# Local and global attention with a three-way max layer: the first 16 tiles written stage by stage and issued in that order, large tiles at one place modulo 256 bytes

## The chip, the cores and the metric

The kernel runs on one core of a Trainium2 chip. The metric is the device time of one execution in microseconds (us). Before the change three runs took 868.49, 871.20 and 872.62 us, median 871.2. One more execution was recorded by the hardware profiler.

## The reference

For 8 batches and 8 heads of width 64 there are 512 local tokens and 32 global ones. A global token attends to all 544 tokens, a local one to the 32 global tokens and to the local tokens within 32 positions. Two softmaxes, one output, then a layer with three first matrices and a maximum over them:

```python
s_g = scale * np.matmul(q_g, k_all.transpose(0, 1, 3, 2))
out_g = np.matmul(sm(s_g), v_all)
s_ll = np.where(np.abs(pos[:, None] - pos[None, :]) <= 32, scale * q_l @ k_l.T, -1e9)
s_l = np.concatenate([s_lg, s_ll], axis=-1)
out_l = np.matmul(sm(s_l), np.concatenate([v_g, v_l], axis=2))
x = concat([out_g, out_l], axis=2) -> [8 * 544, 512]
h = np.maximum(np.maximum(x @ w1, x @ w2), x @ w3)      # 512 -> 768
out = h @ w_out                                         # 768 -> 512
```

All inputs and outputs are fp32.

## The kernel before

A *tile* `sl` is 128 local queries of one pair of heads: 4 tiles (`t` = 0 to 3) make a pair `p`, 4 pairs a batch `b`, so there are 128 tiles, 16 to a batch. The work on one tile has these stages:

- `scores` (lines 290 to 322): four matmuls of queries and keys into PSUM (L305 for the first 28 tiles, L309 later); on DVE, for each of the two heads, a fused mask, scale and row minimum that reads PSUM (L312); on ACT the exponential with its row sum (L314); on DVE 1e-9 added and the reciprocal (L316, L317); the scaling `times` (mostly on POOL, L110); and a DMA that lays the result into `early` or `prob` (L320).
- `trans` (L332): four PE transposes of that tile into PSUM `T`, copied to `pt` by ACT or DVE.
- `transg` (L350): one transpose of the global softmax, copied into the same `pt`.
- `pv` (L370, later L377): the matmuls with the values into PSUM `O`, copied to `xr`; after the fourth tile of a pair a sum over `xr` (L387).
- `glob`, `glob_soft`: once a pair, the scores of the global queries in two halves (L263, L271), their softmax (L279 to L282) and six DMAs into `probg` (L288).
- `split_x`: once a pair, `xr` is split into a rounded part and its remainder, `xs` (a copy on ACT or DVE, a subtraction on POOL or DVE, L92).

`moe_group` is the dense layer of one batch: for each of six column blocks `f`, 36 matmuls of 512 columns (L408: rounded weights `wh` with both parts of `xs`, remainders `wl` with the first), then the maximum on DVE (L416) and a split `h`; then 72 matmuls with `woh` and `wol` (L427). The generator `fill(n)` puts n of these matmuls between the stages of the tiles of the *next* batch, 18 to a tile. So the layer of batch 0 runs beside tiles 16 to 31.

The weights come as 64-bit numbers in 24 pieces (18 of w1 to w3, then 6 of w_out). `convert` makes one piece into its two parts: an absolute value on ACT (L165), four DVE instructions over 512 columns (L166 to L169), a rounded copy `wh` on DVE or ACT and a subtraction `wl` on POOL. `weight_step` advances two pieces by one of these phases each and starts the DMA of another; the list `WS` says how many such steps follow each tile.

The names `copy`, `sub` and `times` choose the engine by counts of spent nanoseconds (`least`), at lines 98 and 100, 92, and 106 to 110. The order in which an engine's instructions stand is not the order of the program text: the framework's scheduler sorts what the text issues, by a model of when it can start. Each engine then works through its queue in order.

PSUM has 8 banks: three for `pm` (the dense layer, and the scores of the first 12 tiles), two for `S` (other scores, `transg`, `glob`), one for `T` and two for `O`. In SBUF most large tiles begin 32 bytes past a multiple of 256; the ones that are allocated after the small tiles `nm` and `z` begin 160 bytes past.

Of the kernel before, what the change touches and what calls it, by code (L numbers as in the profile page):

```python
# [51 lines left out]
def body(ctx, tc, kin, qin, vin, min_, w1, w2, w3, w4, out):  # L52
    nc = tc.nc
    act, dve, pool, pe = nc.scalar, nc.vector, nc.gpsimd, nc.tensor
# [8 lines left out]
    psO = ctx.enter_context(tc.tile_pool(name="psO", bufs=1, space=PSUM))  # L63

# [51 lines left out]
    mask = const.tile([128, 2, 224], BF16, name="mask")  # L116
    zero = const.tile([128, 1], F32, name="zero")
# [38 lines left out]
    def convert(piece):  # L156
# [3 lines left out]
        nc.sync.dma_start(out=r.rearrange("p (k f) -> p k f", k=k) if k > 1 else r, in_=src)  # L160
# [39 lines left out]
    EARLY, AHEAD = 16, 9  # L200
    kraw, kst, qraw, qs, vraw, vs, xr, sc, pg, pts = [{} for _ in range(10)]

    def load_k(p):
        if p < B * NP:
            if 4 * p in NATK:
                kraw[p] = att.tile([128, KW + 2 * SG], F32, name="kn", tag="kst")
            else:
                kraw[p] = att.tile([128, KW + 2 * SG], F32, name="kraw", bufs=1)
            nc.sync.dma_start(out=kraw[p], in_=kin[p])
# [15 lines left out]
    def load_q(s):  # L225
        if s < NS:
# [4 lines left out]
            nc.sync.dma_start(out=qraw[s], in_=qin[s])  # L231
# [8 lines left out]
    def load_v(s):  # L240
        if s < NS:
            vraw[s] = att.tile([128, 4, D], F32, name="vraw", bufs=3)
            nc.sync.dma_start(out=vraw[s], in_=vin[s].rearrange("p (x d) -> p x d", d=D))
# [8 lines left out]
    def glob(p, step):  # L252
        if p >= B * NP:
            return
        if step == 0:
            pg[p] = [att.tile([64, NG], F32, name="sg", bufs=1), att.tile([64, 2], F32, name="nmg"), att.tile([64, 2], F32, name="zg")]
# [3 lines left out]
        ps = psS.tile([128, 512], F32, name="S")  # L260
# [4 lines left out]
        else:  # L265
            for j in range(2):
# [4 lines left out]
        dve.tensor_tensor_reduce(out=s[:, s0:s0 + n], in0=ps[0:64, 0:n], in1=in1, scale=-0.125, scalar=3.0e38,  # L271
                                 op0=ALU.add, op1=ALU.min, accum_out=nm[:, step:step + 1])
        spend("d", n * 1.04 + 75)

    def glob_soft(p):
# [4 lines left out]
        act.activation(out=s, in_=s, func=AF.Exp, bias=nm[:, 0:1], scale=-1.0, accum_out=z[:, 0:1])  # L280
        dve.tensor_scalar(out=z[:, 0:1], in0=z[:, 0:1], scalar1=1e-9, scalar2=None, op0=ALU.add)
        dve.reciprocal(out=z[:, 0:1], in_=z[:, 0:1])  # L282
        spend("d", 220)
        spend("a", 760)
        times(s, s, z[:, 0:1])

        for c0, n, i, h, d0 in GPUT:
            nc.sync.dma_start(out=f32(probg[p % 2])[64 * h:64 * h + 64, i, d0:d0 + n], in_=s[:, c0:c0 + n])  # L288

    def scores(sl):  # L290
        if sl >= NS:
            return
# [3 lines left out]
        ps = pm.tile([128, 512], F32, name="pm") if sl < 12 else psS.tile([128, 512], F32, name="S")  # L296
        s = att.tile([128, 2, 224], F32, name="s", bufs=4)
        sc[sl] = early[:, sl % 6] if sl < EARLY else prob[sl % 2]
        nm = att.tile([128, 2], F32, name="nm")
        z = att.tile([128, 2], F32, name="z")  # L300
        ph = [ps[:, 0:224], ps[:, 224:448]]
        for j in range(2):
# [5 lines left out]
            for a in range(2):  # L308
                pe.matmul(ph[j][:, 0:n], lhsT=qs[sl][:, a, 128 * j:128 * j + 128],  # L309
                          rhs=kst[p][:, j, c0:c0 + n], start=(a == 0), stop=(a == 1))  # L310
        for j in range(2):
# [3 lines left out]
                           accum_out=z[:, j:j + 1])  # L315
        dve.tensor_scalar(out=z, in0=z, scalar1=1e-9, scalar2=None, op0=ALU.add)  # L316
# [3 lines left out]
        nc.sync.dma_start(out=f32(sc[sl])[:, :, 0:n], in_=s[:, :, 0:n])  # L320
        spend("d", 2 * (n * 1.04 + 75) + 150)
        spend("a", 2 * (n * 0.833 + 278))
# [115 lines left out]
    def moe_local(b):  # L438
        def st(t, o):
            r = b * TOK + SG + t * 128  # L440
            nc.sync.dma_start(out=out[r:r + 128], in_=o)
        return moe_group(xs.pop(b), SL, st)

    def moe_glob():
        t = [split_x(xg[:, k], 256) for k in range(NP)]

        def st(i, o):
            for c in range(4):
                r = (4 * i + c) * TOK
                nc.sync.dma_start(out=out[r:r + SG], in_=o[32 * c:32 * c + 32])  # L450
# [4 lines left out]
    WS = [0, 0, 0, 1, 0, 1, 0, 1, 0, 1, 0, 1, 2, 2, 1, 2, 2, 1, 2, 2, 1, 2, 2, 1, 2, 2]  # L455
# [8 lines left out]
    def next_scores(last):  # L464
        while ahead[0] <= last:
            scores(ahead[0])
# [3 lines left out]

    load_k(0)
    load_q(0)
    mraw = cut[:, 5, 0:448].bitcast(F32)
    nc.sync.dma_start(out=mraw, in_=min_.rearrange("p t c -> p (t c)"))
    dve.tensor_copy(out=mask.rearrange("p t c -> p (t c)"), in_=mraw)
    load_q(1)
    load_q(2)
# [101 lines left out]
```

## Time and profile before

| | |
|---|---|
| three runs | 868.49, 871.20, 872.62 us (median 871.2) |
| the profiled execution | 873.07 us |
| its span, first to last instruction | 871.3 us |
| PE busy, and idle in the span | 817.7 us (94%), 53.6 us |
| DVE, ACT, POOL busy | 614.3, 492.2, 504.6 us |

A profile is read here by its stages. "Busy" is the time in which at least one instruction of the engine runs. PEld is the loading of the stationary operand, which overlaps PE. A row of a timeline holds the start, the length, the engine, the source line, the operation, its output and inputs, and in brackets the idle time of the engine just before it and what ended that. PEclk is the share of TensorE's full clock that was granted. Line numbers are those of the kernel before.

### The profile page before, as it was taken

How to read it: one execution, taken by the hardware profiler on the slowest of the kernel's cores; microseconds unless marked ns; L12 is line 12 of the kernel's file. 1: busy time of each engine (PE TensorE's matmuls, PEld its weight loads, DVE VectorE, ACT ScalarE, POOL GpSimd, SP SyncE). 2: the span in 40 equal slices, each digit the busy share in tenths (PEclk: the TensorE clock that was granted, in tenths of full speed). 3: DMA queues.
4: the chain of work that ended last, by engine and by line, in shares of the span. 5: the costliest groups of instructions: out<-in, count | busy, mean ns of one | idle time of the engine just before them, and what ended most of it. 6: DMA issues, size and time to landing. Idle time of an engine off the chain costs nothing.

```text
span 871.3 us, 15748 instructions
## 1 busy us (share of the span) xinstructions
PE 817.7 (94%) x4452; PEld 674.0 (77%) x4452; DVE 614.3 (71%) x1885; ACT 492.2 (56%) x1392; POOL 504.6 (58%) x669
## 2 busy tenths in 40 slices
PE   5875788899999999999999999999999999999997
PEld 4553566688888888888888888888888888888896
DVE  5577788887778787887788887877887877521111
ACT  4555455566666666666676667676666665411111
POOL 4444666685667666776667566756676664411211
PEclk8798799899999999999999999999999999999999
DMA  6567564534333533343334423353334321100001
GB/s 215 172 191 220 176 209 129 160 95 142 100 99 103 164 104 110 99 136 118 95 103 120 134 90 109 90 158 110 104 110 135 117 85 61 69 15 1 25 25 25
DMA packets 107239, 98.54 MB, mean 113 GB/s; under 512 B 21008, under 2 KB 97936, under 8 KB 107152
## 3 DMA queue, kind: packets, MB, share of 16 engines
q1 hardware_dynamic: 107152, 97.53, 36.8%
q8 instruction: 36, 0.59, 0.3%
q14 instruction: 51, 0.42, 0.2%
HBM read 56.85 MB, written 8.91 MB: 75 GB/s over the span
## 4 chain that ended last, share of the span: by engine, by line
PE 79%; DVE 9%; DMA 4%; POOL 3%; issue 3%; ACT 1%; SPq 0%; DVEq 0%; ACTq 0%; POOLq 0%
PE pm L408 46%; PE pm L427 14%; PE O L377 6%; PE S L309 5%; PE T L332 4%; DMA wraw<-w_in 2%; PE S L267 1%; PE S L305 1%; PE O L370 1%; DMA wraw<-wo_in 1%; DVE wraw L168 1%; POOL wl L92 1%; PE S L350 1%; DVE xs L98 1%; DMA early<-s 1%
## 5 line engine op out<-in xcount | busy, mean ns | idle before, releaser
L408 PE MATMUL pm<-xs,wh 128*128 128x512 f32 (+1 forms) x1296 | 412.6, 391 | 16.1 <-POOL xs L92 8.8
L408 PEld LDWEIGHTS pm<-xs,wh 128*128 128x128 f32 x1296 | 234.7, 190 | 52.4 <-POOL xs L92 10.5
L408 PE MATMUL pm<-xs,wl 128*128 128x512 f32 (+1 forms) x648 | 255.1, 394 | 0.5 <-POOL wl L92 0.5
L110 POOL TENSOR_SCALAR s<-s,z 128x224 f32<-128x224 f32 (+1 forms) x243 | 110.0, 465 | 89.1 <-ACT lox L100 48.7
L314 ACT ACTIVATE s<-s,nm 128x192 f32<-128x192 f32 (+1 forms) x256 | 118.0, 462 | 51.2 <-DVE nm L312 26.9
L408 PEld LDWEIGHTS pm<-xs,wl 128*128 128x128 f32 x648 | 123.4, 190 | 24.1 <-issue 1.0
L427 PE MATMUL pm<-woh,h 128*128 128x512 f32 x408 | 136.0, 401 | 1.2 <-POOL h L92 1.1
L92 POOL TENSOR_TENSOR h<-m,h 128x512 fp32r<-128x512 f32 (+1 forms) x54 | 69.0, 1278 | 96.2 <-ACT h L100 96.2
L92 POOL TENSOR_TENSOR qs<-qraw,qs 128x256 fp32r<-128x256 f32 x100 | 78.7, 787 | 69.1 <-ACT qs L100 40.4
L416 DVE TENSOR_TENSOR m<-pm,m 128x512 f32<-128x512 f32 (+1 forms) x108 | 71.0, 658 | 65.5 <-PE pm L408 65.4
L92 DVE TENSOR_TENSOR pt<-T,pt 128x512 fp32r<-128x512 f32 x102 | 70.4, 691 | 34.3 <-ACT pt L100 32.4
L427 PEld LDWEIGHTS pm<-woh,h 128*128 128x128 f32 x408 | 74.7, 188 | 16.0 <-POOL h L92 4.3
L312 DVE CUSTOM_DVE_ANT_0 s<-S,mask 128x192 f32<-128x192 f32 (+1 forms) x232 | 77.6, 370 | 12.1 <-PE S L305 7.7
L427 PE MATMUL pm<-wol,h 128*128 128x512 f32 x204 | 82.0, 402 | 0.0
L92 POOL TENSOR_TENSOR vs<-vraw,vs 128x256 fp32r<-128x256 f32 x102 | 75.8, 743 | 8.9 <-ACT vs L100 3.9
L100 ACT CAST pt<-T 128x512 fp32r<-128x512 f32 x83 | 48.6, 586 | 47.7 <-PE T L332 47.5
L377 PEld LDWEIGHTS O<-pt,vs 128*128 128x128 f32 x408 | 66.9, 188 | 9.1
L377 PE MATMUL O<-pt,vs 128*128 128x320 f32 (+1 forms) x408 | 73.4, 301 | 0.0
L100 ACT CAST qs<-qraw 128x256 fp32r<-128x256 f32 x85 | 34.5, 406 | 65.6 <-PE S L309 61.9
L309 PEld LDWEIGHTS S<-kst,qs 128*128 128x128 f32 x400 | 59.7, 190 | 11.5 <-DVE nmg L271 2.8
L316 DVE TENSOR_SCALAR z<-z 128x2 f32<-128x2 f32 x128 | 40.6, 317 | 38.0 <-ACT s L314 34.7
L100 ACT CAST h<-m 128x512 fp32r<-128x512 f32 (+1 forms) x54 | 32.3, 598 | 61.1 <-DVE m L416 61.0
(99 smaller groups left out, 1344.8 us busy)
## 6 DMA issues: line engine op xcount, KB each, us to landing
vraw<-v_in SPq DMA_DIRECT2D x128, 128.0 KB, 2.4
qraw<-q_in SPq DMA_DIRECT2D x100, 128.0 KB, 2.2
prob<-s SPq DMA_DIRECT2D x56, 224.0 KB, 2.5
prob<-s SPq DMA_DIRECT2D x56, 192.0 KB, 2.3
wraw<-w_in SPq DMA_DIRECT2D x18, 512.0 KB, 4.8
out_dram<-o SPq DMA_DIRECT2D x32, 256.0 KB, 2.5
kraw<-k_in SPq DMA_DIRECT2D x25, 320.0 KB, 3.0
qn<-q_in SPq DMA_DIRECT2D x28, 128.0 KB, 3.1
```

Of the source, the lines that this page charges most:

```text
L92: (dve if least(c) == "d" else pool).tensor_tensor(out=out, in0=a, in1=b, op=ALU.subtract)
L100: act.copy(out=out, in_=a)
L110: pool.tensor_scalar(out=out, in0=a, scalar1=col, scalar2=1.0, op0=ALU.mult, op1=ALU.mult)
L309: pe.matmul(ph[j][:, 0:n], lhsT=qs[sl][:, a, 128 * j:128 * j + 128], rhs=kst[p][:, j, c0:c0 + n], start=(a == 0), stop=(a == 1))
L312: dve.tensor_tensor_reduce(out=s[:, j, 0:n], in0=ph[j][:, 0:n], in1=mask[:, (1, 0, 1, 0)[t], 32 * (t == 0):32 * (t == 0) + n], scale=-0.12 ...
L314: act.activation(out=s[:, j, 0:n], in_=s[:, j, 0:n], func=AF.Exp, bias=nm[:, j:j + 1], scale=-1.0, accum_out=z[:, j:j + 1])
L316: dve.tensor_scalar(out=z, in0=z, scalar1=1e-9, scalar2=None, op0=ALU.add)
L332: pe.transpose(pr[:, 256 * j + 128 * c:256 * j + 128 * c + 128], s[:, j, 128 * c:128 * c + 128], identr)
L377: pe.matmul(o[:, j, 0:320].rearrange("p (a q) -> p a q", a=2)[:, :, 0:n], lhsT=vs[sl][:, 2 * j + c].rearrange("p a d -> p (a d)"), rhs=pt[ ...
L408: pe.matmul(ps[:, 0:n], lhsT=w[f][:, i, k], rhs=xs[k][:, a, 0:n], start=(q == 0), stop=(q == 11))
L416: dve.tensor_tensor(out=m[:, 0:n], in0=ps[:, 0:n], in1=m[:, 0:n], op=ALU.max)
L427: pe.matmul(ps, lhsT=hh[f][:, a, 128 * t:128 * t + 128], rhs=w[:, f], start=(q == 0), stop=(q == 17))
```

## The change

It has two parts.

The first is an order. Every engine handle becomes an `Engine` object. While `strict[0]` is true it keeps each instruction on its engine in the order of the text, and it remembers the last instruction of each engine. `scores` is cut into `score_products` (the matmuls), `score_exp` (mask, minimum, exponential) and `score_norm` (reciprocal, scaling, DMA), `glob_soft` into `glob_exp` and `glob_norm`, and the DVE half of `glob` can be put off through the list `later`. The loop over the first 16 tiles is written anew. At tile `sl` it issues the transposes of tile `sl+1`, then `step()` (normalise the tile whose exponentials were issued one step before, exponentials of the tile whose products were issued last, then the put-off halves of `glob`), the products of tile `sl+5`, `weight_step`s, the values of tile `sl`, `glob`, and the global transpose of tile `sl+1`. After the 16 tiles `strict[0]` becomes false, and everything later is placed behind the last strict instruction of its engine (`issue_after`). So no matmul of the dense layer can stand ahead of the end of this block. The scores of the first 16 tiles and their `glob` take their PSUM from `pm`; 20 tiles instead of 16 use `early`. `WS` has 10 steps instead of 12 in the first 16 tiles, and 16 instead of 17 from tile 16 on.

The second part is a place. The small tiles `nm`, `z`, `nmg`, `zg` and `zero` move to a pool `small` at the end of SBUF, with four buffers instead of two for the first four; `mask` is padded to 256 columns and `sg` to 576. All large tiles then begin 128 bytes past a multiple of 256.

```diff
+    strict = [True]
+    last = {}
+    class Engine:
...
+            def g(*args, **kw):
+                i = f(*args, **kw)
+                if strict[0]:
+                    tc.keep_in_program_order(i)
+                    last[self.name] = i.ins
+                return i
...
+    small = ctx.enter_context(tc.tile_pool(name="small", bufs=4))
-    mask = const.tile([128, 2, 224], BF16, name="mask")
+    mask = const.tile([128, 2, 256], BF16, name="mask")
-    EARLY, AHEAD = 16, 9
+    EARLY = 20
-        ps = psS.tile([128, 512], F32, name="S")
+        ps = pm.tile([128, 512], F32, name="pm") if later is not None else psS.tile([128, 512], F32, name="S")
-        ps = pm.tile([128, 512], F32, name="pm") if sl < 12 else psS.tile([128, 512], F32, name="S")
+        ps = pm.tile([128, 512], F32, name="pm") if sl < 16 else psS.tile([128, 512], F32, name="S")
-        nm = att.tile([128, 2], F32, name="nm")
-        z = att.tile([128, 2], F32, name="z")
+        nm = small.tile([128, 2], F32, name="nm")
+        z = small.tile([128, 2], F32, name="z")
-    WS = [0, 0, 0, 1, 0, 1, 0, 1, 0, 1, 0, 1, 2, 2, 1, 2, 2, 1, 2, 2, 1, 2, 2, 1, 2, 2]
+    WS = [0, 0, 1, 1, 1, 0, 1, 1, 1, 0, 1, 1, 1, 0, 1, 0, 1, 1, 2, 1, 1, 2, 1, 1, 2, 1, 1, 1, 1]
+    def step():
+        for sl in exped:
+            score_norm(sl)
+        exped.clear()
+        for sl in made:
+            score_exp(sl)
+            exped.append(sl)
+        made.clear()
+        for r in reds:
+            r()
+        reds.clear()
...
+    for sl in range(16):
+        p, t = divmod(sl, 4)
+        settle(4500)
+        trans(sl + 1)
+        step()
+        if t == 2:
+            glob_exp(p + 1)
+        new_scores(min(sl + 5, EARLY - 1), products)
...
+        for _ in range(WS[sl]):
+            weight_step()
+        pv(sl)
+        if t <= 1:
+            glob(p + 1, t, reds)
+        elif t == 2:
+            glob_norm(p + 1)
+        transg(sl + 1)
+        split_v(sl + 2)
+        load_v(sl + 3)
+        if t == 3:
+            split_pair(p)
+    step()
+    step()
+    strict[0] = False
+    for i in last.values():
+        ctx.enter_context(tc.issue_after(i))
+    for sl in range(16, NS):
```

The rows that follow are instructions in the order in which they stand in an engine's queue: source line, operation, output and inputs, shape, and a count. In the changed kernel every line reads L66, the line of the wrapper.

DVE, in the first tiles: before, around the second weight piece (`cut`, `wraw`).

```order
L317 RECIPROCAL z<-z 128x2
L312 ISA s,nm<-pm,mask 128x224
L312 ISA nm 128x1
L167 TENSOR_SCALAR cut<-cut 128x512
L168 SCALAR_TENSOR_TENSOR wraw<-wraw,cut 128x512
L98 COPY pt<-T 128x4x128
L316 TENSOR_SCALAR z<-z 128x2
L169 SCALAR_TENSOR_TENSOR cut<-wraw 128x512
L317 RECIPROCAL z<-z 128x2
```

DVE, changed kernel, tile 6 of the loop (exponentials of tile 10, second half of the global scores, then a piece):

```order
L66 ISA s,nm<-pm,mask 128x224
L66 ISA nm 128x1
L66 ISA sg,nmg<-pm,zero 64x160
L66 ISA nmg 64x1
L66 TENSOR_TENSOR nmg<-nmg 64x1
L66 CAST wh_102<-cut 128x512
L66 TENSOR_SCALAR cut<-cut 128x512 x2
L66 SCALAR_TENSOR_TENSOR wraw<-wraw,cut 128x512
L66 SCALAR_TENSOR_TENSOR cut<-wraw 128x512
L66 TENSOR_SCALAR zg<-zg 64x1
```

The four instructions of a piece, which stood between those of other tiles, now stand together behind the minima of one tile.

ACT, before, around the second pair's global softmax and the third piece:

```order
L280 ACTIVATE sg,zg<-sg,nmg 64x544
L100 COPY pt<-S 128x2x32
L100 COPY pt<-T 128x4x128
L100 COPY pt<-S 128x2x2x32
L165 ACTIVATE cut<-wraw 128x512
L100 COPY xr<-O 128x160
```

ACT, changed kernel, tile 6 of the loop:

```order
L66 ACTIVATE s,z<-s,nm 128x224 x2
L66 ACTIVATE sg,zg<-sg,nmg 64x544
L66 ACTIVATE cut<-wraw 128x512
L66 COPY xr<-O 128x160
L66 COPY pt<-S 128x2x2x32
L66 COPY pt<-T 128x4x128
```

The absolute value of a weight piece now stands directly behind the exponentials of the same step.

PE, before, at the end of batch 0's tiles (`T<-identr,prob_89` is tile 16):

```order
L305 MATMUL S<-kn,qn 128x224 x2
L370 MATMUL O<-pt,vraw 64x160 x4
L332 MATMUL T<-identr,prob_89 128x128 x4
L408 MATMUL pm<-xs,wh_99 128x512 x2
L332 MATMUL T<-identr,prob_90 128x128 x4
L408 MATMUL pm<-xs,wl_105 128x512
```

PE, changed kernel, at the end of the strict block (`T<-identr,early` in the last transpose row is tile 17):

```order
L66 MATMUL O<-pt,vraw 64x160 x4
L66 MATMUL S<-identr,probg_94 128x128
L66 MATMUL T<-identr,early 128x128 x4
L66 MATMUL pm<-xs,wh_102 128x512 x2
L66 MATMUL pm<-xs,wl_108 128x512
```

Before, 30 matmuls of the dense layer stand ahead of tile 16's values; now none does. From the transposes of tile 23 on the two PE queues read alike to the end.

More of the change, by code (lines that the diff above doesn't have):

```diff
@@ L115, in body @@
     dve.tensor_copy(out=identr, in_=one)
-    mask = const.tile([128, 2, 224], BF16, name="mask")
-    zero = const.tile([128, 1], F32, name="zero")
+    mask = const.tile([128, 2, 256], BF16, name="mask")
+    zero = small.tile([128, 1], F32, name="zero", bufs=1)
     dve.memset(zero, 0.0)
@@ L242, in load_v @@
             vraw[s] = att.tile([128, 4, D], F32, name="vraw", bufs=3)
-            nc.sync.dma_start(out=vraw[s], in_=vin[s].rearrange("p (x d) -> p x d", d=D))
+            sp.dma_start(out=vraw[s], in_=vin[s].rearrange("p (x d) -> p x d", d=D))
     def split_v(s):
@@ L250, in split_v, with glob @@
             sub(t[:, :, 1], v, f32(t)[:, :, 0])
-    def glob(p, step):
+    def glob(p, step, later=None):
         if p >= B * NP:
@@ L255, in glob @@
         if step == 0:
-            pg[p] = [att.tile([64, NG], F32, name="sg", bufs=1), att.tile([64, 2], F32, name="nmg"), att.tile([64, 2], F32, name="zg")]
+            pg[p] = [att.tile([64, KW], F32, name="sg", bufs=1)[:, 0:NG], small.tile([64, 2], F32, name="nmg"), small.tile([64, 2], F32, name="zg")]
         s, nm, z = pg[p]
@@ L270, in glob, with red, glob_exp @@
             copy(in1, ps[64:128, 0:n], True)
[L271 to L275, printed above, removed]
+        def red():
+            dve.tensor_tensor_reduce(out=s[:, s0:s0 + n], in0=ps[0:64, 0:n], in1=in1, scale=-0.125, scalar=3.0e38,
+                                     op0=ALU.add, op1=ALU.min, accum_out=nm[:, step:step + 1])
+            spend("d", n * 1.04 + 75)
+        if later is None:
+            red()
+        else:
+            later.append(red)
+    def glob_exp(p):
         if p >= B * NP:
@@ L310, in scores, with score_exp @@
                           rhs=kst[p][:, j, c0:c0 + n], start=(a == 0), stop=(a == 1))
+        st[sl] = s, nm, z, ph
+    def score_exp(sl):
+        t = sl % 4
+        n = WIN[t][1]
+        s, nm, z, ph = st[sl]
         for j in range(2):
@@ L319, in scores @@
             times(s[:, j, 0:n], s[:, j, 0:n], z[:, j:j + 1])
-        nc.sync.dma_start(out=f32(sc[sl])[:, :, 0:n], in_=s[:, :, 0:n])
-        spend("d", 2 * (n * 1.04 + 75) + 150)
-        spend("a", 2 * (n * 0.833 + 278))
+        sp.dma_start(out=f32(sc[sl])[:, :, 0:n], in_=s[:, :, 0:n])
+        spend("d", 150)
     def trans(sl):
@@ L462, in body, with new_scores @@
     ahead = [0]
-    def next_scores(last):
-        while ahead[0] <= last:
-            scores(ahead[0])
+    def new_scores(last, then):
+        while ahead[0] <= min(last, NS - 1):
+            then(ahead[0])
             split_q(ahead[0] + 1)
@@ L496, in body @@
         settle(4500)
-        if sl % 16 == 0 and b:
+        if sl % 16 == 0:
             fill(400)
@@ L510, in body @@
         elif t == 2:
-            glob_soft(p + 1)
+            glob_exp(p + 1)
+            glob_norm(p + 1)
         fill(3)
```

80 lines of the change are left out of this document (54 added, 26 removed).

## The prediction

> **What bounds the kernel now.** I read the page first (busy times, the slices), then the stretches of the span, then the timelines of PE, POOL and DVE in the first 140 us.
>
> ```profile
> span 871.3 us, 15748 instructions
> ...
> PE 817.7 (94%) x4452; PEld 674.0 (77%) x4452; DVE 614.3 (71%) x1885; ACT 492.2 (56%) x1392; POOL 504.6 (58%) x669
> ...
> PE   5875788899999999999999999999999999999997
> ```
>
> PE is full from the ninth slice on. Only the first 8 slices (some 175 us) have room, and a change there is worth what it brings forward of PE's later queue. The next rows cut the rest of the span at three places: the values of tile 16 (98.66), the place from which the two PE queues read alike (137.03, just after the transposes of tile 23), and the first w_out matmul (182.4). The columns are length, then busy time of PE, PEld, DVE, ACT, POOL, then the granted clock.
>
> ```profile
> 98.66:137.03 38.37, 34.12 (x182) 25.04 (x180) 34.10 (x83) 23.29 (x63) 23.97 (x23) 0.94 0.68 212
> 137.03:182.40 45.37, 38.58 (x202) 29.96 (x202) 38.00 (x99) 25.97 (x71) 30.24 (x37) 0.92 0.44 131
> 182.40:871.00 688.60, 681.90 (x3719) 574.48 (x3717) 478.07 (x1483) 393.79 (x1108) 400.14 (x542) 1.00 0.31 95
> ```
>
> PE idles 4.25 us in the first, 6.8 in the second; the last is PE's own work. In the first two DVE is busy 89% and 84%: it nearly sets the pace there. The last idles 6.7, so of the 53.6 us that PE idles in all some 36 lie before 98.66. Where:
>
> ```profile
> 80.39 0.76 PE L370 MATMUL O<-pt,vraw 128*64 128x160 f32 x8 [1.19 <-ACT pt L100]
> 88.93 0.79 PE L408 MATMUL pm<-xs,wh 128*128 128x512 f32 x1 [7.31 <-ACT xs L100]
> 94.19 0.79 PE L408 MATMUL pm<-xs,wh 128*128 128x512 f32 x1 [4.47 <-POOL xs L92]
> 97.43 1.23 PE L370 MATMUL O<-pt,vraw 128*64 128x160 f32 x8
> ```
>
> and on POOL:
>
> ```profile
> 82.63 4.96 POOL L92 TENSOR_TENSOR wl<-cut,wh 128x512 fp32r<-128x512 f32 x2 [3.15 <-ACT wh L100]
> ```
>
> Tile 15's values are done at 81. Then a matmul of the dense layer stands at the head of PE's queue and waits for the last `xs`, behind POOL's weight subtractions; tile 16 waits behind it until 97. The reason is that the weights came late: a piece ends with L169.
>
> ```profile
> L169 DVE SCALAR_TENSOR_TENSOR cut<-wraw x11: 678/691/1650, 16.5 to 93.1; 128x512 int32<-128x512 int32 x11
> ```
>
> Five of these 11 pieces run after 80, while PE idles.
>
> **The change, part by part.** The removed block at 81 to 97 is real, so what counts is when the strict block ends.
>
> *Entry.* PE's first products start when the keys land, the first minima when the mask is cast. The global softmax of pair 0 is scaled on POOL near where it is now; its six DMAs hold SP's queue for 4.63 us, and the row of tile 2 now stands behind them.
>
> ```profile
> 12.30 0.71 POOL L110 TENSOR_SCALAR sg<-sg,zg 64x544 f32<-64x544 f32 x1
> 14.14 4.63 SPq L288 DMA_DIRECT2D probg<-sg  x6
> ```
>
> and, by the DMA issues (KB each, median us to landing),
>
> ```profile
> early<-s SPq DMA_DIRECT2D x8, 192.0 KB, 3.1
> ```
>
> So 12.5 + 4.6 + 3.1 = 20.2 for tile 2's transposes, one light step of 2.5, and loop step 2, the first with weights, starts at about 22.7. The first weight DMA moves on SP's queue too, ahead of the rows of tiles 0 and 1 and of three loads of queries; nothing waits for it before step 2, so I cost that at nothing, and if DMAs are late there each microsecond counts once.
>
> *A step with weights.* DVE's queue is strict, so the minima of a tile come first, ACT's two exponentials follow, ACT's absolute value stands behind those, and only then can DVE's four instructions run. Before, DVE filled this wait with other tiles.
>
> ```profile
> 7.07 0.36 DVE L312 CUSTOM_DVE_ANT_0 s<-pm,mask 128x192 f32<-128x192 f32 x1 [0.53 <-PE pm L305]
> ...
> 8.27 0.19 ACT L314 ACTIVATION_READ_ACCUMULATOR s<-s,nm 128x1 f32 x1
> 10.76 0.73 ACT L280 ACTIVATE sg<-sg,nmg 64x544 f32<-64x544 f32 x1
> 14.15 0.66 ACT L165 ACTIVATE cut<-wraw 128x512 f32<-128x512 f32 x1 [1.64 <-DMA wraw<-w_in]
> 14.84 0.43 DVE L166 TENSOR_SCALAR cut<-cut 128x512 f32<-128x512 f32 x1 [1.61 <-ACT cut L165]
> 16.50 0.69 DVE L169 SCALAR_TENSOR_TENSOR cut<-wraw 128x512 int32<-128x512 int32 x1
> 59.95 0.17 DVE L316 TENSOR_SCALAR z<-z 128x2 f32<-128x2 f32 x1
> ```
>
> From the minima's start to the end of the exponentials 1.3 (7.07 to 8.36), absolute value 0.7, DVE's four 2.35 (14.84 to 17.19), z and a reciprocal like it 0.3: 4.65. Six such steps (tiles 3, 4, 7, 8, 11, 12) are 27.9. In tiles 2, 6, 10 and 14 the global exponential (0.73) stands ahead of the absolute value and some 0.35 of small DVE work is added: 5.75, four times 23.0.
>
> *A light step* (5, 9, 13, 15) is PE's:
>
> ```profile
> 59.66 0.92 PE L305 MATMUL S<-kn,qn 128*128 128x192 f32 x4
> ...
> 61.27 0.50 PE L332 MATMUL T<-identr,early 128*128 128x128 f32 x4
> ```
>
> From the products over the values and the global transpose to the end of the tile's transposes 2.1 (59.66 to 61.77), and some 0.4 for `glob`: 2.5, four times 10.0.
>
> *Extras.* Three copies of `T` stand on DVE, two rounded copies on ACT ahead of the absolute value, three sums over `xr`: 2.0 + 1.0 + 0.9. And after every fourth tile POOL's `xs` meets DVE's integer instructions, which take two SBUF inputs:
>
> ```profile
> 65.52 1.65 DVE L169 SCALAR_TENSOR_TENSOR cut<-wraw 128x512 int32<-128x512 int32 x1
> ...
> 65.19 1.43 POOL L92 TENSOR_TENSOR xs<-xr,xs 128x512 fp32r<-128x512 f32 x1 [1.40 <-ACT xs L100]
> 86.38 1.49 DVE L166 TENSOR_SCALAR cut<-cut 128x512 f32<-128x512 f32 x1
> ```
>
> 0.69 alone (the row at 16.50), 1.65 beside POOL: 0.96 more per meeting, three times 2.9 at most; I take 2.0. A `wl` subtraction can hold up L166 by up to 1.06 in the same way (the last row, against 0.43 at 14.84); it should mostly have ended before the absolute value is there, so I take zero, with 10 x 1.06 as the upper end.
>
> Sum: 22.7 + 27.9 + 23.0 + 10.0 + 3.9 + 2.0 = 89.5 for the end of the strict block; bounds 82 (no meetings, and the overlap of the first rival below) and 100 (every `wl` meets L166).
>
> *What follows.* Up to the place where the queues agree, PE now has 30 dense matmuls more than before (at 0.24, below), and tile 16's values and tile 17's transposes (1.0):
>
> ```profile
> 210.69 1.68 PE pm L408 x7
> ```
>
> 7.2 + 1.0 on top of 38.4 is 46.6 if PE idles as before. DVE's work there is the same eight pieces in a longer stretch, 34.1 in some 44 instead of in 38.4, so I take 3 of the 4.25 idle back: 43.6 (bounds 42.3 and 46.6). 89.5 + 43.6 = 133.1 against 137.03: 3.9 earlier. From tile 16 on `WS` asks for four pieces in three tiles where it asked for five, which spares some of the 6.8: I take 1.5 (0 to 5). Together 5.4.
>
> *The place modulo 256* I cost at nothing: no tile of before lies at the new place in one use and elsewhere in another. The nearest rows: the weights of L408 (`wh`, at 32) load in 190 ns, those of L427 (`h`, at 160) in 188.
>
> ```profile
> L408 PEld LDWEIGHTS pm<-xs,wh 128*128 128x128 f32 x1296 | 234.7, 190 | 52.4 <-POOL xs L92 10.5
> L427 PEld LDWEIGHTS pm<-woh,h 128*128 128x128 f32 x408 | 74.7, 188 | 16.0 <-POOL h L92 4.3
> ```
>
> 1% of that either way in all PE's steady work would be 7 us, which is the bound. Four buffers for `nm` and `z` free waits on small tiles that no row shows.
>
> 873.07 - 5.4 = 867.7 in the profiled execution's time (span 865.9). That execution lies 1.9 above the median of the runs, so 866 against 871.2.
>
> **The rivals.**
> - *The front is faster* (0.16): the steps overlap more than in my chain. A heavy step leaves DVE busy in about 3.7 of 4.65 us, 79%; the stretch from 98.66 shows that it can be busy 89%. At that the loop's 66.8 us become 59.3, the block ends at 82, and the kernel takes 858. DVE's waits for ACT in a strict queue speak against it.
> - *Slower: PE at half clock in the front* (0.22). Without dense matmuls PE is busy about half of each step. At half clock the four products take
>
> ```profile
> 95.91 1.59 PE L305 MATMUL S<-kn,qn 128*128 128x192 f32 x4
> 35.00:40.00 5.00, 2.76 (x7) 1.94 (x9) 1.92 (x8) 2.13 (x9) 3.87 (x8) 0.52 0.43 126
> 37.24 0.79 PE L408 MATMUL pm<-xs,wh 128*128 128x512 f32 x1 [2.27 <-POOL xs L92]
> ```
>
> 1.59 instead of 0.92, a factor of 1.73. The light steps grow by 1.8 each, 7 in all, and ACT's copies wait for PE ahead of the next exponentials: PE's 2.1 in a heavy step becomes 3.6, and I estimate 0.5 of that uncovered, ten times 5. Block end 101.5, 878. It decides from an end of 95 (no gain) and 99 (slower).
> [...]
> - *The conversions set the end* (0.17): before, the last of 24 pieces ends at 171 us, 13 pieces after 94, so 5.9 us each.
>
> ```profile
> L169 DVE SCALAR_TENSOR_TENSOR wct<-wraw x6: 675/686/1712, 133.7 to 170.3; 128x512 int32<-128x512 int32 x6
> ```
>
> Now 14 instead of 13 are left; at 5.9 each they end at 89.5 + 83 = 172, as late as now, and PE waits for them: 871.
> - *The forecast* (0.45).
>
> **How the numbers follow.** A measurement of this kernel can tell about 0.5%, 4.4 us, from no change. The forecast's own range is 861 to 871. The range to hold 8 of 10 cases reaches a little past the fast rival and the slow one, 854 to 879. Faster by over 0.5%: the fast rival and four fifths of the forecast, 0.16 + 0.36 = 0.52. Within: the rest of the forecast and the third rival, 0.26. Slower: 0.22.
>
> **What would show it.** The block's end: the last transposes of a global row ahead of the first dense matmul, at 84 to 95, and from there dense matmuls without a wait for `xs`. DVE's four instructions of a piece in one run behind about 1 us of idle that ACT's absolute value ends. PEclk in the first four slices: 0.8 to 0.9 for me, 0.5 to 0.6 for the half clock. The transposes of tile 23 at about 132. PE idle after them below 5 us up to the first w_out matmul; if it is 7 or more, the conversions set it. The forecast is wrong if PE's durations change in the steady part (then the place matters) or if the first tiles wait for DMAs that I have at their present latency.

## The result, and the profile after

The changed kernel takes 883.34 us (median of four runs, 881.53 to 886.46) against 869.85 for the kernel before on the same chip: ratio 1.0156, 95% interval 1.0113 to 1.0199. It is 1.6% slower, above the whole range that was forecast (854 to 879). The profiled execution took 881.53, with a span of 879.3. The lines of the page of after that answer to those shown of before:

```profile
span 879.3 us, 15705 instructions
...
PE 816.4 (93%) x4452; PEld 674.4 (77%) x4452; DVE 612.7 (70%) x1869; ACT 488.1 (56%) x1399; POOL 499.9 (57%) x678
...
PE   4656696999999999999999999999999999999997
...
PEclk8777798999999999999999999999999999999999
```

PE has the same work (816.4 busy against 817.7) and idles 62.9 us of the span instead of 53.6. Most of that is in the first eight slices, `46566969` where before had `58757888`: PE idles 53.1 us in them against 46.6. How far behind PE is can be read from the work that it has left at one late moment. Stretches of the span after (length, busy time of PE with the number of its matmul records in brackets, granted clock, DMA share, GB/s):

```profile
0.00:102.00 102.00, 58.63 (x318) 0.76 0.60 181
...
142.00:190.00 48.00, 40.75 (x214) 0.93 0.38 112
...
700.00:880.00 180.00, 174.78 (x949) 1.00 0.13 41
```

and before:

```profile
0.00:102.00 102.00, 66.41 (x371) 0.82 0.64 193
...
700.00:880.00 180.00, 166.57 (x889) 0.99 0.11 35
```

By these records PE has issued 53 matmuls fewer at 102 us and has been busy 7.8 us less, and at 700 it has 8.2 us more left to do. So the loss is there at 102 us and does not come back by 700.

What PE waits for most there, from the list of waits of after up to 102 us (us in total, times, longest):

```profile
PE S L66 <- DMA probg<-sg: 30.5, 5, 6.8
```

The transposes of the global rows stand in PE's queue ahead of everything of the next tile, and at each of five pair boundaries they wait about 6 us for `probg`. Why it comes late, in the timeline of tile 2 (start, length, engine; the wait before it in brackets):

```profile
30.43 0.74 ACT L66 ACTIVATE sg<-sg,nmg 64x544 f32<-64x544 f32 x1
...
31.16 0.65 ACT L66 ACTIVATE cut<-wraw 128x512 f32<-128x512 f32 x1
31.84 0.89 DVE L66 TENSOR_SCALAR cut<-cut 128x512 f32<-128x512 f32 x2 [1.52 <-ACT cut L66]
33.49 0.69 DVE L66 SCALAR_TENSOR_TENSOR cut<-wraw 128x512 int32<-128x512 int32 x1
34.10 0.14 DVE L66 TENSOR_SCALAR zg<-zg 64x1 f32<-64x1 f32 x1
34.67 0.71 POOL L66 TENSOR_SCALAR sg<-sg,zg 64x544 f32<-64x544 f32 x1 [4.65 <-DVE z L66]
35.41 3.69 SPq L66 DMA_DIRECT2D probg<-sg  x6
39.14 0.34 PE L66 MATMUL S<-identr,probg 128*128 128x128 f32 x1 [6.18 <-DMA probg<-sg]
39.79 1.82 PE L66 MATMUL pm<-kn,qn 128*128 128x224 f32 x4
```

The global exponentials end at 31.2, but their sum is taken at 34.10, since DVE's queue holds the whole weight piece first, and the piece waits 1.52 for ACT. Then come POOL, six issues on SP (3.69), and PE at 39.14. On DVE the waits from 22 to 94 us are led by the absolute value:

```profile
DVE cut L66 <- ACT cut L66: 14.0, 10, 3.0
```

Ten waits, one for each piece. The block ends here:

```profile
100.92 0.34 PE L66 MATMUL S<-identr,probg 128*128 128x128 f32 x1 [5.70 <-DMA probg<-sg]
101.06 0.71 PE L66 MATMUL T<-identr,early 128*128 128x128 f32 x4
101.57 1.18 PE L66 MATMUL pm<-xs,wh 128*128 128x512 f32 x2
```

at 101.57, where 89.5 was forecast, 1.6 above the upper bound of 100.

### The profile page after: what moved, and what is told of

The parts are those of the page before. It is cut to its first block, busy times and chain, and to the rows that moved or that the text cites. A ratio compares the mean times of both kernels' runs of the same rounds, so it can differ in the third digit from the quotient of the medians.

```text
span 879.3 us, 15705 instructions
## 1 busy us (share of the span) xinstructions
PE 816.4 (93%) x4452; PEld 674.4 (77%) x4452; DVE 612.7 (70%) x1869; ACT 488.1 (56%) x1399; POOL 499.9 (57%) x678
## 4 chain that ended last, share of the span: by engine, by line
PE 76%; DVE 10%; DMA 5%; ACT 3%; SPq 2%; issue 2%; POOL 2%; DVEq 0%; ACTq 0%; POOLq 0%
PE pm L66 59%; PE S L66 7%; PE O L66 6%; PE T L66 3%; DVE cut L66 2%; SPq L66 2%; DMA wraw<-w_in 1%; DVE wraw L66 1%; ACT s L66 1%; DVE kst L66 1%; DMA probg<-sg 1%; DVE z L66 1%; DMA qn<-q_in 1%; DVE s L66 1%; DMA vraw<-v_in 1%
## 5 line engine op out<-in xcount | busy, mean ns | idle before, releaser
L66 PE MATMUL pm<-xs,wh 128*128 128x512 f32 (+1 forms) x1296 | 409.1, 389 | 0.0
L66 PEld LDWEIGHTS pm<-xs,wh 128*128 128x128 f32 x1296 | 234.5, 190 | 31.6
L66 PE MATMUL pm<-xs,wl 128*128 128x512 f32 (+1 forms) x648 | 254.3, 392 | 0.0
L66 POOL TENSOR_SCALAR s<-s,z 128x192 f32<-128x192 f32 (+1 forms) x254 | 111.9, 453 | 94.8 <-ACT lox L66 51.6
L66 ACT ACTIVATE s<-s,nm 128x192 f32<-128x192 f32 (+1 forms) x256 | 118.0, 462 | 66.5 <-DVE nm L66 63.5
L66 PEld LDWEIGHTS pm<-xs,wl 128*128 128x128 f32 x648 | 123.1, 190 | 23.5 <-issue 2.2
L66 PE MATMUL pm<-woh,h 128*128 128x512 f32 x408 | 134.0, 399 | 0.0
L66 POOL TENSOR_TENSOR h<-m,h 128x512 fp32r<-128x512 f32 (+1 forms) x54 | 68.2, 1263 | 99.0 <-ACT h L66 99.0
L66 DVE TENSOR_TENSOR m<-pm,m 128x512 f32<-128x512 f32 (+1 forms) x108 | 71.1, 658 | 67.5 <-PE pm L66 67.2
L66 POOL TENSOR_TENSOR qs<-qraw,qs 128x256 fp32r<-128x256 f32 x99 | 77.3, 781 | 59.1 <-ACT qs L66 39.3
L66 DVE TENSOR_TENSOR pt<-T,pt 128x512 fp32r<-128x512 f32 x102 | 70.4, 690 | 32.5 <-ACT pt L66 30.4
L66 PEld LDWEIGHTS pm<-woh,h 128*128 128x128 f32 x408 | 74.6, 188 | 12.6 <-POOL h L66 1.3
L66 POOL TENSOR_TENSOR vs<-vraw,vs 128x256 fp32r<-128x256 f32 x102 | 76.0, 745 | 12.9 <-DVE vs L66 6.7
L66 PE MATMUL pm<-wol,h 128*128 128x512 f32 x204 | 81.7, 401 | 0.0
L66 DVE CUSTOM_DVE_ANT_0 s<-S,mask 128x192 f32<-128x192 f32 (+1 forms) x224 | 74.5, 370 | 6.7 <-PE S L66 2.2
L66 PEld LDWEIGHTS O<-pt,vs 128*128 128x128 f32 x408 | 66.4, 188 | 9.1
L66 ACT CAST qs<-qraw 128x256 fp32r<-128x256 f32 x86 | 35.0, 407 | 68.7 <-PE S L66 67.8
L66 PE MATMUL O<-pt,vs 128*128 128x320 f32 (+1 forms) x408 | 72.8, 300 | 0.0
L66 DVE TENSOR_SCALAR z<-z 128x2 f32<-128x2 f32 x128 | 43.8, 342 | 40.2 <-ACT s L66 39.4
L66 ACT CAST pt<-T 128x512 fp32r<-128x512 f32 x77 | 44.8, 582 | 48.3 <-PE T L66 48.3
L66 PEld LDWEIGHTS S<-kst,qs 128*128 128x128 f32 x400 | 59.3, 189 | 14.8 <-DVE nmg L66 6.3
L66 POOL TENSOR_TENSOR kst<-kraw,kst 64x576 fp32r<-64x576 f32 x44 | 66.6, 1514 | 6.9 <-DVE nm L66 2.8
```

What stands on the lines that cost most here:

```text
L66: i = f(*args, **kw)
```

## The experiments

In each entry the ratio is to the kernel before, run in the same comparison (its medians there lay between 869.96 and 871.43); "after" stands at 1.0156. Microseconds won or lost are between medians, against 883.34; since the kernel before itself had medians up to 1.6 us apart, differences of a microsecond or two mean nothing. Intervals are those of 95%.

### First theory: PE's waits for probg

**norm_first**: the global sums ahead of the piece on DVE.

```
+        if t == 2:
+            glob_norm(p + 1)
         for _ in range(WS[sl]):
             weight_step()
...
-        elif t == 2:
-            glob_norm(p + 1)
```

> The changed kernel with one edit: in the third tile of a pair, the sums of the global softmax (zg) are taken on VectorE ahead of that tile's piece of the weight conversion instead of behind it. The trace of after has the global exp ending at 31.26 and zg only at 34.10 to 34.27, so the copies into probg can start about 2.8 us earlier in each of the four later pairs. Theory (TensorE waits for probg at every pair boundary, 5.6 to 6.8 us each): each of these waits shrinks by about 2.8, the strict block ends at about 90 instead of 101.5, and the kernel takes about 872 (869 to 876). Rival 1 (TensorE at half clock in the front sets the block's end by itself): the block ends less than 3 us earlier, 880 or more. Rival 2 (the conversions set the end): the block ends earlier, the first w_out matmul does not, 881 to 884.

Measured: 880.56, ratio 1.0113 (1.0096 to 1.0131). A miss of the theory; the numbers are those of rival 1. The waits did shrink,

```profile
PE S L66 <- DMA probg<-sg: 20.0, 5, 5.6
```

by 10.5 us in all, but the first dense matmul came only 1.5 us earlier (100.11), and the time fell by some 3, with intervals that overlap. Whether that is the half clock, "warm" below tests.

**no_probg**: no copies into `probg` for pairs 1 to 4.

```
-        for c0, n, i, h, d0 in GPUT:
+        for c0, n, i, h, d0 in GPUT if not 1 <= p <= 4 else ():
```

> The changed kernel without the copies of the global softmax's rows into probg for pairs 1 to 4 (that part of the computation is left out, the sums and exponentials stay). Theory: the waits of 6.84, 6.18, 6.21, 5.61 and 5.70 us vanish but for what the softmax itself takes behind the copies of the scores; the block ends at 78 to 86 and the kernel takes 862 to 870. Rival 1 (half clock): the block still ends behind 93, 876 or more. Rival 2 (the conversions set the end): the block ends at about 80, but the first w_out matmul stays within 3 us of 193.4, 880 to 884.

Measured: 875.89, ratio 1.0058 (1.0039 to 1.0078): 7.5 us. This lies between the theories, at the edge of rival 1 (876 or more, an end behind 93); "warm" below is the test of that rival. PE's waits in the first 102 us:

```profile
PE O L66 <- ACT pt L66: 7.1, 5, 2.8
PE pm L66 <- DVE nm L66: 7.0, 3, 2.8
PE S L66 <- DMA probg<-sg: 6.5, 1, 6.5
```

24 us of waiting are gone (the entry's 6.5 is left), others for DVE and ACT stand in their place, and the first dense matmul comes at 94.71, 6.9 earlier. The pieces on DVE tell why. One instruction of the pieces of tiles 6 and 14, after:

```profile
54.03 0.69 DVE L66 SCALAR_TENSOR_TENSOR wraw<-wraw,cut 128x512 int32<-128x512 int32 x1
...
94.57 0.69 DVE L66 SCALAR_TENSOR_TENSOR wraw<-wraw,cut 128x512 int32<-128x512 int32 x1
```

and without the copies:

```profile
54.95 0.69 DVE L66 SCALAR_TENSOR_TENSOR wraw<-wraw,cut 128x512 int32<-128x512 int32 x1
...
94.11 0.69 DVE L66 SCALAR_TENSOR_TENSOR wraw<-wraw,cut 128x512 int32<-128x512 int32 x1
```

Eight tiles take 40.5 us with the waits and 39.2 without them, some 20 for four. So something else keeps that pace (the runs with DVE released, below, show what), and PE's waits at the first boundaries lay beside it. Of the 6.9 us, 6.4 are won behind the last of these pieces: only the last wait, behind which the block ends, was on the path.

**glob_tile_earlier**: both halves of the global scores in a pair's first tile, exponentials and sums in its second.

```
-        if t == 2:
+        if t == 1:
             glob_exp(p + 1)
...
+        if t == 1:
+            glob_norm(p + 1)
...
-        if t <= 1:
-            glob(p + 1, t, reds)
-        elif t == 2:
-            glob_norm(p + 1)
+        if t == 0:
+            glob(p + 1, 0, reds)
+            glob(p + 1, 1, reds)
```

> The changed kernel, nothing left out, with the global softmax of the next pair one tile earlier: both halves of the global scores in the first tile of a pair, exponentials and sums in the second, so that the copies into probg have a whole tile more (about 5 us) before TensorE's strict queue stands at the transposes of their rows. Theory: the waits fall from about 6 to about 1 each, the block ends at 80 to 88, the kernel takes 864 to 872. Rival 1 (half clock): the block ends behind 95, 878 or more. Rival 2 (conversions): the block ends early, the first w_out matmul stays at about 193, 880 to 884.

Measured: 871.94, ratio 1.0018 (1.0002 to 1.0034). The time is as expected, the way to it is not: the first dense matmul comes at 98.58, not at 80 to 88, with new waits,

```profile
PE pm L66 <- DVE nm L66: 11.7, 5, 4.0
PE S L66 <- DMA probg<-sg: 6.7, 2, 5.6
```

and most of the gain is made behind the block. By the matmul records PE is 12 ahead of after at 102 us, 22 at 142 and 45 at 190; from 142 to 190 it is busy 44.11 us against 40.75:

```profile
142.00:190.00 48.00, 44.11 (x237) 0.96 0.47 147
```

Why that stretch runs better was not followed up. The end of the block alone does not rank the kernels: 98.58 goes with 871.94 here, 97.52 with 878.3 in "both_entry" below.

### Rival: PE at half clock

**warm**: twelve matmuls of zeros in PE's wait at each pair boundary.

```
+        if t == 3:
+            g = psS.tile([128, 512], F32, name="S")
+            for _ in range(12):
+                pe.matmul(g, lhsT=identr, rhs=prob[1]..., start=True, stop=True)
         transg(sl + 1)
```

> The changed kernel with twelve extra matmuls of zeros of 512 columns ahead of the transposes of the global rows at each pair boundary, where TensorE waits 5.6 to 6.8 us for probg (their results are not used). At 0.22 to 0.45 us each they take 2.6 to 5.4, inside the wait. Rival (half clock in the front costs the time): the granted clock of the first 101.5 us rises above 0.85, the products behind the waits fall from 1.8 to 0.9, and the kernel takes 875 to 879. Theory (the waits themselves): only the four products behind each wait get shorter, and these are partly covered, so the block ends at most 4 us earlier and the kernel takes 880 to 884.

Measured: 881.8, ratio 1.0133 (1.0098 to 1.0167), within the intervals no gain, as the theory has it. The granted clock did rise (0.76 to 0.83 over the first 101.5 us), and the products behind the wait at 39 us, 1.82 in after, took 0.99:

```profile
39.62 0.25 PE L66 MATMUL S<-identr,probg 128*128 128x128 f32 x1 [3.26 <-DMA probg<-sg]
40.09 0.99 PE L66 MATMUL pm<-kn,qn 128*128 128x224 f32 x4
```

but the first dense matmul stayed at 101.76 (101.57 in after). So a mean clock of 0.83 instead of 0.76 brought the block's end no earlier. Three limits: 0.83 is the clock that before has in its first 102 us (0.82), not the full one; the wait for `probg` at the entry has no added matmuls; and behind two of the four filled waits PE was slow all the same (the transposes at 61.59 took 0.72 us, against 0.51 at 39.74; the products at 82.22 took 1.86).

### Second theory: DVE's wait for ACT

**abs_ahead**: ACT takes a piece's absolute value one weight step earlier.

```
         act.activation(out=f32(c), ..., func=AF.Abs)
+        spend("a", 520)
+        yield
...
             next(live[0])
+            absed[0] = False
+            if strict[0] and loaded:
+                next(loaded[0])
+                absed[0] = True
```

> The changed kernel with one edit: inside the first 16 tiles ScalarE takes the absolute value of a weight piece one weight step earlier, so VectorE's strict queue no longer stands behind it (in after: 10 waits, 14.0 us between 22 and 94 us). Theory now (two waits of equal standing: TensorE for probg and VectorE for ScalarE; leaving out the probg copies alone gave 7.5 us): the waits for the absolute value vanish, but since the probg waits go on covering them, the block ends 3 to 7 us earlier than 101.5 and the kernel takes 876 to 880. Rival (probg waits alone bound the block): no change, 882 to 885. Rival (half clock): no change either.

Measured: 879.5, ratio 1.0102 (1.0068 to 1.0137). The time is as expected, 3.8 us less by the medians, though the interval overlaps that of after. Of DVE's ten waits one is left (1.5 us), and PE still waits 27.0 for `probg`. But the first dense matmul comes at 99.65, 1.9 earlier and not 3 to 7, and the fourth and the tenth piece lie 39.2 us apart, against 40.5. So DVE's waits for ACT are not by themselves what keeps the pace.

**both**, **both_entry**: this edit and glob_tile_earlier together; then a piece in the first tile as well:

```
-    WS = [0, 0, 1, 1, 1, ..., 1, 1, 2, 1, ...
+    WS = [1, 0, 1, 1, 1, ..., 1, 1, 1, 1, ...
```

> The two edits together: global softmax one tile earlier, absolute value one weight step earlier. Nothing left out. Theory: in the kernel with the first edit alone the loop of a heavy step is scores on VectorE, four ScalarE instructions 0.98, absolute value 0.57, four VectorE instructions 2.65, sums and the next scores, 5.1 in all; the second edit takes 1.55 us out of this loop, 9 times, so the block ends at 84 to 89 instead of 98.4; the kernel takes 862 to 867 against 871.9 with the first edit alone. Rival (half clock): the block does not move by more than 3, 869 to 872. Rival (the conversions of the next stretch set the end): the block ends early, the kernel still takes 868 to 872.

> The same two edits, and a weight step already in the first tile, where VectorE idles (first piece of before at 15.8 us, of after at 32.8), one fewer behind tile 18. Theory: one piece of 2.65 us less on VectorE where TensorE has dense work to do; 1 to 4 us less than the two edits alone. Rival (the block's end sets it): the piece lengthens the block by as much, no change or up to 2 us more.

Measured: 875.74, ratio 1.0058 (1.0037 to 1.0079), and 878.3, ratio 1.0083 (1.0049 to 1.0117). Both fail, theory and rivals: the two edits together are worse than the better one alone (871.94), and a piece at the entry makes it no better (the intervals overlap). The first dense matmul comes at 100.03 and 97.52, not at 84 to 89. A new wait leads PE's queue of "both" up to 102 us,

```profile
PE T L66 <- DMA early<-s: 10.7, 4, 3.6
```

and another DVE's: three waits of 8.3 us in all for ACT's copies `xr`, ahead of the sums `xg`. With every queue fixed, taking one wait away let the next one stand. That speaks for a third theory: not a certain wait, but the fixing.

### Third theory: the pinned order itself

**free_order**, **free_glob**, **strict8**: the code as written, but nothing pinned (the diff); the same with glob_tile_earlier; pinned only up to tile 7 (`strict[0] = False` at the end of tile 7).

```
-    strict = [True]
+    strict = [False]
```

> The changed kernel as written, placement included, but the first 16 tiles not pinned to program order: each engine's instructions are ordered as in the rest of the kernel. TensorE then has transposes and products of later tiles ahead of the transposes of the global rows. Theory (the pinned order itself, in which every engine stands behind whatever is late: probg, the absolute value, cold products): probg waits fall below 8 us in all, the kernel takes 866 to 872. Rival (the written order, with scores made a tile ahead and glob in halves, asks for more by itself): 876 to 884 with the waits at other names.

> The kernel with the global softmax one tile earlier (871.9 when pinned), not pinned. Theory (pinned order): 864 to 869, since one more late transfer is out of the way. Rival: within 2 us of the pinned one, 870 to 874.

> The changed kernel with the first 8 tiles pinned and tiles 8 to 15 written alike but not pinned. Theory (pinned order): about half of what the unpinned kernel gains, the probg waits at the first three pairs stay and the others go: 873 to 879. Rival (written order): 881 to 885.

Measured: free_order 867.75, ratio 0.9961 (0.9940 to 0.9982); free_glob 866.91, ratio 0.9946 (0.9916 to 0.9976); strict8 873.5, ratio 1.0027 (1.0011 to 1.0043). All three as the theory has it, and the first two are faster than both kernels, by 0.4 and 0.5% of the kernel before. The page of free_order:

```profile
PE   5878997879999999999999999999999999999997
```

Among PE's waits up to 102 us none is for `probg`; the longest is 5.4 us, for a `wl` of POOL. DVE waits 1.9 us for the absolute value, where the pinned kernel waits 14.0, and the last instruction of its pieces reads

```profile
L66 DVE SCALAR_TENSOR_TENSOR cut<-wraw x18: 675/686/1649, 18.0 to 127.8; 128x512 int32<-128x512 int32 x18
```

The first piece is at 18.0 us where the pinned kernel has it at 33.49, and PE's first dense matmul stands at 64 us, inside what was the block. Unpinned, the kernel also loses the bar that kept the dense layer behind the block, since `issue_after` goes by the instructions that were pinned.

**pe_free**, **pe_pinned**, **dve_free**: all engines pinned but PE (the diff); PE alone pinned (`== "t"`); all but DVE (`!= "d"`). An engine that is not pinned has no bar at the block's end either.

```
-                if strict[0]:
+                if strict[0] and self.name != "t":
```

> The changed kernel with every engine but TensorE pinned in the first 16 tiles. Theory (TensorE's strict queue is what costs): it may run transposes and products of later tiles while the copies into probg are under way; 868 to 873, most of the 15.6 us between after and the unpinned kernel. Rival (VectorE's strict queue costs): VectorE still waits some 14 us for the absolute values, 878 to 883. If each has a half: 873 to 878.

> The changed kernel with TensorE alone pinned. Theory (TensorE's queue): the probg waits stay above 20 us in all, 877 to 883. Rival (VectorE's queue): 868 to 872, as unpinned. If each has a half: 872 to 877.

> The changed kernel with every engine but VectorE pinned. Theory (TensorE's queue): 878 to 883, VectorE's waits for the absolute value go down and those of TensorE for probg stay. Rival (VectorE's queue): 868 to 874.

Measured: pe_free 874.34, ratio 1.0023 (1.0004 to 1.0043); pe_pinned 869.96, ratio 1.0007 (0.9983 to 1.0030); dve_free 870.72, ratio 0.9997 (0.9972 to 1.0022). The theory of PE's queue falls: pe_free is where each would have a half, the other two are where the rival had them. With PE alone pinned, its bar included, 13.4 of the 15.6 us are won back, and freeing DVE alone wins 12.6 us although PE's queue keeps its order. PE's waits of dve_free up to 102 us begin with

```profile
PE S L66 <- DMA probg<-sg: 18.4, 5, 7.4
```

so PE still stands for `probg`. But DVE waits only 2.6 us for the absolute value, and the loop is shorter. PE is pinned in both kernels, so its transposes of a global row at the first and the last boundary show the pace; in after they start at 21.02 (the last, at 100.92, is shown above),

```profile
21.02 0.34 PE L66 MATMUL S<-identr,probg 128*128 128x128 f32 x1 [6.84 <-DMA probg<-sg]
```

and in dve_free:

```profile
23.91 0.34 PE L66 MATMUL S<-identr,probg 128*128 128x128 f32 x1 [7.36 <-DMA probg<-sg]
...
89.38 0.34 PE L66 MATMUL S<-identr,probg 128*128 128x128 f32 x1 [3.18 <-DMA probg<-sg]
```

Sixteen tiles take 65.5 us instead of 79.9, four take 16.4 instead of 20.0 (16.5 in pe_pinned, from 22.22 to 88.23), and the first dense matmul comes at 90.02. In pe_free the opposite holds: DVE keeps its waits for ACT,

```profile
DVE cut L66 <- ACT cut L66: 13.6, 10, 1.8
```

and its 20 us for four tiles (40.1 from the fourth piece to the tenth), yet 9.0 us are won: PE moves its first dense matmul to 73.24, inside the block. So the long loop comes with DVE's fixed queue, the empty time in it can be filled only if PE is free, and either release is worth more than half: the two (12.6 and 9.0) come to more than the 15.6 of freeing every engine. Order and bar fall together in these runs; the shorter loop of dve_free lies inside the block, where no bar stands, while the gain of pe_free needs both. Which of DVE's instructions has to move up stays open.

### The second part of the change

**place_only**: the kernel before with the small tiles, mask and `sg` of the change. **order_only**: the changed kernel without them (four buffers for `nm` and `z` kept). **free_noplace**: free_order without them. The core of place_only, which order_only takes back:

```
-    mask = const.tile([128, 2, 224], BF16, name="mask")
+    mask = const.tile([128, 2, 256], BF16, name="mask")
...
-        nm = att.tile([128, 2], F32, name="nm")
+        nm = small.tile([128, 2], F32, name="nm")
```

> The kernel before with the second part of the change alone: the pool of small tiles with two buffers, the wider mask and sg, so that large tiles lie at one place modulo 256 bytes. Theory: no effect, ratio to before 0.998 to 1.002, and the weight loads of the two dense products stay at 190 and 188 ns. Rival: the 685.9 against 688.9 us from the first w_out matmul to the end, after against before, come from the place; then this kernel is 3 us (0.35%) or more faster than before.

> The changed kernel without its second part: small tiles, mask and sg lie as before (the four buffers for nm and z stay). The second part alone made the kernel before 0.3% (2.6 us) faster. Theory (the two parts add): 2 to 4 us slower than after, 885 to 888. Rival (placement acts only with the order of before): 882 to 885.

> The unpinned kernel (867.75) with small tiles, mask and sg as before, so without the second part of the change. If its 0.39% over before is the placement: ratio 0.998 to 1.002 to before, 869.5 to 872.5. If it is the written order: 0.994 to 0.998, 866 to 869. The matmuls of the dense products show no difference in either case by more than 2 ns.

Measured: place_only 868.47, ratio 0.9970 (0.9950 to 0.9990); order_only 883.25, ratio 1.0130 (1.0093 to 1.0167); free_noplace 868.18, ratio 0.9968 (0.9947 to 0.9988). In both orders of this code, pinned and not, the second part makes no difference that can be told (883.25 beside 883.34, 868.18 beside 867.75). With the order of before it comes out 0.3% faster (1.8 us by the medians), between the theory's range and the rival's 3 us, at the edge of what can be told. In after, with the same places, the weight loads are no shorter than in before: `wh` in 190 ns and `h` in 188 in both. From the first w_out matmul to the end the profiles (one execution each) of after and place_only take 685.9 and 686.0 us against 688.8 in before; but order_only, with the places of before, takes 685.3, so the place is not needed for these 3 us. free_order's gain over before does not need the placement either: the rest of the change (the written order, `WS`, the PSUM tiles), unpinned, brings it.

## Why the prediction was wrong

**The place was right.** The steady part kept its durations (products with `wh` 389 ns against 391), and the loss lies ahead of the first w_out matmul, which starts 10.9 us later (193.42 against 182.48). The placement at nothing was right for the kernel after.

**The first step that failed: the end of the strict block**, 22.7 + 27.9 + 23.0 + 10.0 + 3.9 + 2.0 = 89.5, measured 101.57. Of the 12.1 us:

- *Entry, 5.7.* The sum put the start of the six copies into `probg` at 12.5, which is no row's, and put nothing for SP's queue ahead of them. In after they start at 15.30:

```profile
12.97 0.71 POOL L66 TENSOR_SCALAR sg<-sg,zg 64x544 f32<-64x544 f32 x1 [1.03 <-DVE zg L66]
15.30 4.68 SPq L66 DMA_DIRECT2D probg<-sg  x6
```

  The scaling ends at 13.68, and five loads, one of them of a weight piece, hold SP's queue until 15.21. Then one light step of 2.5 was counted behind the DMAs, with tile 2's transposes at 20.2. PE stood already with tile 0's global row and tile 1's transposes: 21.16, tile 2's at 25.97, tile 3's at

```profile
28.41 0.51 PE L66 MATMUL T<-identr,early 128*128 128x128 f32 x4
```

  28.41, where loop step 2 begins, against 22.7: two light steps behind the six DMAs, the first of them 4.8 us long. The granted clock is 0.51 in that first step, and its products and values take 1.82 and 1.23 us, in the next 0.99 and 0.76; no run takes this apart.
- *The steps, 6.4.* From 28.41 to 101.57 the loop took 73.2 instead of 66.8. Three periods of four tiles (32.77 to 94.57 by the pieces) took 61.8; by my terms they are 3 x (2 x 4.65 + 5.75 + 2.5) = 52.7, and with their share of the extras (5.9 over 14 steps, 12 of them) 57.7: 4.1 too little. The chain of a step (minima, exponentials, absolute value, four instructions) is there: DVE waits 14.0 us for ACT in ten pieces. (Its exponentials were read as ending at 8.36; the row shown ends at 8.46, 0.1 more a step.) But it is not what sets the pace: abs_ahead took these waits away and the block ended 1.9 us earlier, while freeing DVE's whole queue took four tiles from 20.0 to 16.4. What the sum has no term for is that nothing else can run meanwhile. By the order of the queues, ACT's copies for PE stand behind the absolute value, DVE's copy of `T` behind the piece, and PE's next products behind these; which of these costs how much, no run shows.
- *The last wait* is part of the other 2.3 of these 6.4. `probg` was costed at the entry alone, but PE stood for it at each pair boundary, 24 us in all behind the entry. Leaving the copies out moved the block's end by 6.9, 6.4 of it at the last boundary.

**The second step that failed: what follows the block.** 43.6 us (bounds 42.3 and 46.6) were forecast from its end to the transposes of tile 23 (133.1). They came at 153.3, 51.8 us behind the block's end: 8.2 too long, and with the block's 12.1 some 20.2 too late. The forecast left PE 1.25 us idle there, by taking 3 of 4.25 back; it idles 9.5. Most of that is three waits for DVE, and DVE and ACT wait in turn (list of waits from 101.57 to 153.5 us):

```profile
PE S L66 <- DVE nm L66: 8.1, 3, 5.7
...
DVE cut L66 <- ACT cut L66: 8.2, 5, 3.9
...
ACT cut L66 <- DMA wraw<-w_in: 6.4, 4, 3.1
```

So the term that was mis-sized is this idle time, by 8.2 us. Why the pieces run so there was not tested; glob_tile_earlier, whose edit touches only the 16 tiles, has 44.5 us for the same stretch.

From there to the first w_out matmul PE then idled hardly at all,

```profile
153.50:193.40 39.90, 38.43 (x211) 0.97 0.40 116
```

1.5 us; DVE is busy 28.8 of these 39.9 us. The same stretch of before:

```profile
135.80:182.40 46.60, 39.01 (x207) 0.93 0.43 128
```

7.6 of idle, with DVE busy 39.2 of 46.6. The forecast took 1.5 of these back and some 6 came back, which no term of it foresaw: PE came late, and DVE had room. So the stretch from tile 23 to the first w_out matmul takes 40.1 us where 43.9 were forecast, and the rest 3 us less than in before: the 20.2 us too late become the 13.4 by which the span (879.3) misses the forecast's 865.9.

**The rivals.** The half clock forecast a block end of 101.5 and 878, and the block did end there; by what warm shows that is a coincidence, since filling PE's waits at the four later boundaries raised the granted clock of the first 101.5 us from 0.76 to 0.83, left the end where it was and won no time that can be told (1.5 us). What the full clock would give there, no run shows. In after the four products behind the wait of 6.18 us took 1.82; in warm they took 0.99 behind a wait of 3.26 with the dummy matmuls ahead of it, but 1.86 behind one of 2.49 with the same matmuls ahead. The last section has more such places. The conversions as the bound fall by the idle time just shown, and the last piece's start does not rank the kernels: 170.1 us in free_order and 174.9 in free_glob, which is no slower. The fast front (an end at 82, 858) is refuted by the pinned kernel; the unpinned one is faster than before, but takes 867.75. That this lies near the forecast's 866 is luck: the forecast was for the pinned order. The rival that was missing is that the change does what it says on each engine at once: a queue that may not be passed.

**The signs.** Of those named, dense matmuls without a wait for `xs` and DVE's four instructions in one run behind a wait for ACT were as described. PE's idle time behind tile 23 was below 5, as named. The block's end and tile 23 came later than named, and PEclk at 0.7 to 0.8 lay between the two cases.

## What to carry to other kernels

A wait in a list is worth what the loop around it leaves: 24 us of PE's waits were worth 7.5, because four tiles took 20 us on DVE without them too. When instructions are pinned to program order, cost the round trip through all engines for one step, and at the entry count how many steps stand behind the first late DMA. Where such a loop cannot be shortened, leave one engine's queue free to run other work in it: freeing DVE alone gave back 12.6 of 15.6 us, PE alone 9.0.

## What the runs showed of the hardware

The granted clock was low also behind shorter waits than those for `probg` (5.6 to 6.8 us), and in one place not at once. In after, from 44.87 on:

```profile
44.87 0.76 PE L66 MATMUL O<-pt,vraw 128*64 128x160 f32 x8
48.24 0.49 PE L66 MATMUL pm<-kn 128*64 128x160 f32 x2 [2.61 <-DVE nm L66]
...
49.12 0.98 PE L66 MATMUL pm<-kn,qn 128*128 128x192 f32 x4
50.03 1.23 PE L66 MATMUL O<-pt,vraw 128*64 128x160 f32 x8
...
51.87 1.53 PE L66 MATMUL pm<-kn,qn 128*128 128x192 f32 x4
53.46 0.76 PE L66 MATMUL O<-pt,vraw 128*64 128x160 f32 x8
```

After a wait of 2.61 us the first products still took 0.98; 1.8 us later, with PE busy, the values took 1.23 instead of 0.76 and the next products 1.53, and by 53.46 it was over. The granted clock of that stretch (length, PE busy, clock, DMA share, GB/s):

```profile
50.03:53.46 3.43, 3.37 (x18) 0.54 0.58 180
```

In pe_free PE was slow right behind a wait of 2.57 us that ended at 64.56: the products at 65.83 took 1.61, the values at 67.37 took 1.23. In after the granted clock is 0.51 from 70.23 to 73.50, behind a wait of only 1.21. What lowers the clock no run isolates; in these places the length of the wait alone does not tell.
